# A decode kernel on one core: alignment branches ahead of the opening barrier on ScalarE, GpSimd and VectorE

## The chip, the cores and the metric

The kernel runs on one core of a Trainium2 chip. The metric is the device time of one execution in microseconds (us). Most executions of a kernel agree within 0.3%, but there is a second, slower state: here about 444.7 us instead of 436.4 us. Runs are compared fast with fast. The trace also gives a *span*, from the first to the last recorded instruction.

## The reference, cut to what matters

```python
mod = silu(c) @ w_mod                                  # (8, 1024) @ (1024, 6144): six modulation rows
h = layernorm(x) * (1 + ca) + sa
x = x + ga * attention(h, k_cache, v_cache, wq, wo)    # 8 batches, 32 query heads on 4 key heads, 8192 keys of 128
h = layernorm(x) * (1 + cb) + sb
x = x + gb * ((relu(h @ W_gate) * (h @ W_up)) @ W_down)
```

There is one new token per batch, so every weight and every cache entry is read once and used in little arithmetic: 185.6 MB come from HBM, the chip's main memory.

## The kernel before

A small recording layer collects every operation with what it reads and writes, works out the semaphores, and emits one program per engine. SyncE issues all large loads, in order, each as soon as the buffer that it overwrites has been read. The attention over eight batches is a loop on ScalarE, VectorE and TensorE. GpSimd has no loop: its eight products in the attention stand one after another.

The program opens with a barrier of all engines. Two helper steps matter here. The first moves the first loads ahead of that barrier, so that the stream starts at once (its first packet is at 1.01 us, and the barrier opens at 1.42 us):

```python
def start_loads_first(nc, n):
    ...
    for engine, ahead, total in ((mybir.EngineType.SP, 2, n), (mybir.EngineType.Activation, 2, 2)):
        ins = list(block.instructions)
        at = where(ins, engine, "EventSemaphore")[0]
        first = [ins[i] for i in where(ins, engine) if i > at][:total]
        ...
        rest = rest[:at] + first[ahead:] + rest[at:]
        at = where(rest, engine)[0]
        block.instructions = rest[:at] + first[:ahead] + rest[at:]
```

The second emits an engine's code ahead of the loop, and then the loop:

```python
        for x in engines:
            mine = [i for i, o in enumerate(self.ops) if o["eng"] == x]
            inside = [i for i in mine if self.ops[i]["trip"] is not None]
            after[x] = [self.ops[i] for i in mine if inside and i > inside[-1]]
            straight(x, [self.ops[i] for i in mine if not inside or i < inside[0]])
            ...
        with nc.Fori(0, len(self.trips["pe"]), engines=...) as self.turn:   # eight trips
            ...
```

ScalarE's two first loads are the small inputs `c` and `x` (16 KB each, tile `cx`). The first matmul needs both.

## Time and profile before

| what | number | where |
|---|---|---|
| device time, three runs before the prediction | 436.49, 436.64, 444.67 us | run list |
| profiled execution | 444.49 us, span 443.1 us, slow state | run list, page |
| DMA busy, 40 slices | 90% or more in 39 | page |
| share of the load queue | 98.9% of 16 engines' span | page |
| fetches of instructions in the span | five of 16 KiB, one of 8 KiB | packet records |

These lines are from the page of the kernel before, as it was profiled (in the slow state). The DMA row gives tenths of busy time in 40 slices. The queue lines give packets, MB, and the share of the sixteen engines' span.

```profile
span 443.1 us, 4774 instructions
...
DMA  9999999999999999999999999999999999999995
...
q1 hardware_dynamic: 5360, 185.61, 98.9%
q8 instruction: 5, 0.08, 0.1%
...
q14 instruction: 1, 0.01, 0.0%
```

The reader should see two things. The DMA engines are full for the whole span, nearly all of it with the one queue of large loads (q1). And two queues of kind "instruction" move a little as well (0.09 MB): I read these as the programs themselves being fetched.

Next, pieces of the chain of waits of the same profile, in order of time: start in us, duration in us, what.

```profile
381.51 24.74 DMA arena<-in_B_W_gate_dram
...
413.18 26.30 DMA arena<-in_B_W_down_dram
...
439.53 0.61 PE ps L763 x8
...
441.05 0.42 DVE ob L769
```

The chain ends in load landings. Only about 3.6 us of arithmetic and store follow the last landing in it.

The start of the same profile, from its timeline: start us, duration us, engine, line, operation, and in brackets the idle time before it and what ended it (`issue`: nothing that the profile shows; a name with `q`, such as `PEq`: that engine's sequencer, which issues its instructions; `DMA`: a landing).

```profile
0.00 1.44 SPq L391 DMA_DIRECT2D arena<-in_w_mod_dram  x3
0.12 0.40 ACTq L423 DMA_DIRECT2D cx<-in_c_dram  x1
0.23 0.10 POOL L794 MEMSET const-float32-0.0<- 128x1 f32 x1 [0.23 <-issue]
...
0.56 0.44 ACTq L423 DMA_DIRECT2D cx<-in_A_x_dram  x1
1.42 1.28 ACT L451 ACT_TABLE_LOAD   x1 [1.42 <-PEq L794]
...
1.57 0.34 SPq L391 DMA_DIRECT2D arena<-in_A_wq_dram  x1
...
10.03 0.58 PE L447 MATMUL ps<-cx,rsel 32*128 32x512 bf16 x1 [10.03 <-DMA cx<-in_A_x_dram]
```

SyncE queues three loads (12,288 KiB) at once. The barrier opens at 1.42 us, which ScalarE's table load shows. The first matmul waits for the small load of `x` until 10.03 us.

The trace also records each DMA packet. The fetches of instructions, as start in us and size, worked out from those records:

```
8 KiB:   84.7
16 KiB:  50.2  104.2  393.8  410.5  436.6
```

Last, the landing records hold sixteen times for each load, and a wait ends with the last of them. For the small load of `x` the median of the sixteen is 8.18 us and the last 9.94 us, and the matmul that waits for it starts at 10.03 us. For the gate load the median is 404.52 us and the last 406.26 us, and its wait in the chain ends at 406.25 us. I call one of the sixteen a *part*.

### The profile page before, as it was taken

The numbers are of one execution on the slowest core, as the hardware profiler recorded it, in microseconds if no ns is written. First come the engines' busy times: TensorE is split into PE (matmuls) and PEld (weight loads), VectorE is DVE, ScalarE is ACT, GpSimd is POOL, SyncE is SP. The second block draws the span as 40 slices with busy tenths as digits, with TensorE's granted clock in tenths as the row PEclk, the third lists the DMA queues.
The fourth block names the chain that finished last, engine by engine and source line by source line (L and its number), as shares of the span: only waits on it lengthen the run. The fifth ranks groups of instructions, "written<-read, shape, count | busy, mean of one in ns | idle before, by whom it ended". The sixth has DMA issues, their size and how long they took to land. (4 is left out here: it accounts for less than half of the span.)

```text
span 443.1 us, 4774 instructions
## 1 busy us (share of the span) xinstructions
PE 263.3 (59%) x2139; PEld 138.0 (31%) x1979; DVE 249.0 (56%) x342; ACT 29.5 (7%) x54; POOL 8.7 (2%) x22
## 2 busy tenths in 40 slices
PE   0324336728865783886578388658838865365157
PEld 0100002218225421822542172154217215241015
DVE  0603028872985697298569729756972975421020
ACT  1100010020001002000100200010020010100000
POOL 3000000000000000000000000000000000000000
PEclk9976657978996997799599889959968996865668
DMA  9999999999999999999999999999999999999995
GB/s 367 417 355 390 404 385 426 379 417 430 467 396 420 456 444 420 429 470 390 435 476 408 423 429 467 420 423 473 399 420 426 467 455 402 452 416 419 439 414 239
DMA packets 5494, 185.74 MB, mean 419 GB/s; under 512 B 656, under 2 KB 752, under 8 KB 1136
## 3 DMA queue, kind: packets, MB, share of 16 engines
q1 hardware_dynamic: 5360, 185.61, 98.9%
q8 instruction: 5, 0.08, 0.1%
q10 hardware_dynamic: 128, 0.04, 0.0%
q14 instruction: 1, 0.01, 0.0%
HBM read 185.63 MB, written 0.02 MB: 419 GB/s over the span
## 5 line engine op out<-in xcount | busy, mean ns | idle before, releaser
L576 DVE STREAM_TRANSPOSE kt<-arena 128x1024 uint32<-128x1024 uint32 x128 | 148.2, 1211 | 64.4 <-DVEq L181 47.3
L586 PE MATMUL ps<-kt,qpad 128*128 128x512 bf16 x512 | 133.9, 384 | 44.1 <-DVE kt L576 38.1
L626 PE MATMUL ps<-arena,pT 128*64 128x256 bf16 x1024 | 74.5, 320 | 51.8 <-PEq L181 51.8
L626 PEld LDWEIGHTS ps<-arena,pT 128*64 128x64 bf16 x1024 | 72.0, 132 | 53.7 <-issue 53.1
L586 PEld LDWEIGHTS ps<-kt,qpad 128*128 128x128 bf16 x512 | 40.5, 98 | 133.7 <-DVE kt L576 101.0
L616 DVE TENSOR_SCALAR pT<-pd,mqf 128x1024 bf16<-128x1024 bf16 x64 | 28.2, 503 | 0.6
L608 ACT ACTIVATE prb<-ps,bias 128x1024 bf16<-128x1024 f32 x16 | 17.7, 1109 | 139.8 <-DVE mjt L603 139.8
L614 DVE STREAM_TRANSPOSE pd<-prb 128x1024 bf16<-128x1024 bf16 x16 | 19.8, 1239 | 10.9 <-ACT prb L608 10.9
L592 DVE TENSOR_REDUCE negm<-ps 128x1 f32<-128x512 f32 x32 | 21.2, 661 | 4.5 <-PE ps L586 4.5
L744 PE MATMUL ps<-arena,hT 128*32 128x448 bf16 x128 | 11.1, 535 | 16.8 <-DMA arena<-in_B_W_up_dram 11.4
L751 DVE TENSOR_TENSOR kt<-ps,kt 128x448 bf16<-128x448 f32 x2 | 1.2, 618 | 27.6 <-PE ps L744 27.6
L514 PE MATMUL ps<-arena,hT 128*32 128x512 bf16 x96 | 10.3, 615 | 9.7 <-DMA arena<-in_w_mod_dram 9.7
L538 PE MATMUL ps<-arena,hT 128*32 128x512 bf16 x64 | 7.2, 631 | 14.6 <-DMA arena<-in_A_wq_dram 14.6
L645 ACT ACTIVATE oacc<-ps 128x32 f32 (+1 forms) x9 | 1.8, 197 | 159.4 <-PE ps L640 159.4
L521 DVE COPY mod<-ps 128x512 f32<-128x512 f32 x2 | 1.3, 670 | 19.3 <-PE ps L514 19.3
L567 POOL TENSOR_TENSOR qpad<-qR,mq 128x128 bf16<-128x128 bf16 x8 | 4.9, 608 | 319.2 <-DVE pT L616 260.8
L549 DVE CAST kt<-ps 128x512 bf16<-128x512 f32 x1 | 0.7, 691 | 18.2 <-PE ps L538 18.2
L744 PEld LDWEIGHTS ps<-arena,hT 128*32 128x32 bf16 x64 | 2.4, 140 | 25.7 <-DMA arena<-in_B_W_up_dram 12.0
L763 PE MATMUL ps<-arena,hmT 128*32 128x256 bf16 x112 | 8.3, 309 | 3.5 <-DVE hmT L754 3.1
L714 PE MATMUL ps<-arena,kt 128*32 128x256 bf16 x128 | 5.9, 373 | 5.1 <-DMA arena<-in_A_wo_dram 5.1
L598 PE MATMUL ps<-identf,negm 128*128 128x128 f32 x16 | 3.9, 326 | 7.8 <-DVE negm L596 7.8
L763 PEld LDWEIGHTS ps<-arena,hmT 128*32 128x32 bf16 x112 | 6.5, 109 | 5.6 <-DMA arena<-in_B_W_down_dram 4.9
(87 smaller groups left out, 80.9 us busy)
## 6 DMA issues: line engine op xcount, KB each, us to landing
arena<-in_A_k_cache_dram SPq DMA_DIRECT2D x16, 4096.0 KB, 27.5
arena<-in_A_wq_dram SPq DMA_DIRECT2D x2, 4096.0 KB, 38.3
arena<-in_B_W_gate_dram SPq DMA_DIRECT2D x1, 7168.0 KB, 24.7
arena<-in_B_W_up_dram SPq DMA_DIRECT2D x1, 7168.0 KB, 27.9
arena<-in_w_mod_dram SPq DMA_DIRECT2D x1, 6144.0 KB, 33.4
arena<-in_w_mod_dram SPq DMA_DIRECT2D x1, 5888.0 KB, 17.8
arena<-in_B_W_down_dram SPq DMA_DIRECT2D x1, 3584.0 KB, 19.7
arena<-in_B_W_down_dram SPq DMA_DIRECT2D x1, 1792.0 KB, 23.6
```

What stands on the lines that cost most here:

```text
L514: fns.append(lambda e, w=w, pr=pr, j=j, kk=kk: hold(e.matmul(ps[32 * j:32 * j + 32, pr, :], hT[:, kk, :], w[:, 2 * pr:2 * pr + 2, j, :], s ...
L538: fns.append(lambda e, w=w, r=kk - r0, z=z, g=g, kk=kk: hold(e.matmul(ps[32 * g:32 * g + 32, 4 + z, :], hT[:, kk, :], w[:, r, g, z, :], st ...
L576: P.op("dve", lambda e_: e_.transpose(ktb[:, to:to + PART].bitcast(dt.uint32), arena[:, lo:lo + PART].bitcast(dt.uint32)), reads=[slot_r(l ...
L586: fns.append(lambda e_, t=t, r=r: e_.matmul(ps[:, e // 4, :].rearrange("p (c k) -> p c k", k=32), qpad[:, t * 2 + r, 24 - 8 * i:152 - 8 * ...
L592: P.op("dve", lambda e: e.tensor_reduce(negm[:, h:h + 1], ps[:, h, :], AX.X, ALU.max, negate=True), reads=[bank(h)] + (free(("ka", b)) if ...
L608: P.op("act", lambda e: e.activation(prb[:, f, :], ps[:, 2 * f:2 * f + 2, :].rearrange("p h n -> p (h n)"), ACT.Exp, bias=bias[:, 0:1], sc ...
L614: P.op("dve", lambda e: e.transpose(pd[:, f], prb[:, f]), reads=[R("prb", f, f + 1)], writes=[R("pd", 1024 * f, 1024 * f + 1024)])
L616: P.op("dve", lambda e, g=g: e.tensor_scalar(out=pT[:, f, :, :, g, :], in0=pd[:, f].rearrange("p (c i x) -> p c i x", c=32, i=2), scalar1= ...
L626: fns.append(lambda e, n=n, h=h, c_=c_, i=i, t=t: e.matmul(ps[64 * t:64 * t + 64, 5, 0:2 * Dh].rearrange("p (i d) -> p i d", d=Dh), pT[:, ...
L714: fns.append(lambda e, w=w, k=k, j=j: e.matmul(ps[32 * j:32 * j + 32, 5, 0:256], oX[:, k, :], w[:, k, j, :], start=(k == 0), stop=(k == KO ...
L744: fns.append(lambda e, w=w, kk=kk, h=h, j=j, b0=b0: hold(e.matmul(ps[32 * j:32 * j + 32, b0 + h, 0:H], hT[:, kk, :], w[:, kk, j, h, :], st ...
L763: fns.append(lambda e, w=w, r=k - r0, k=k, i2=i2, j=j: e.matmul(ps[32 * j:32 * j + 32, 4, 0:256], hmT[:, k, 1 - i2:33 - i2], w[:, r, i2, j ...
```

## The change

The intent is in its short description: ScalarE, GpSimd and VectorE branch to their next fetch block ahead of their opening-barrier instructions, ScalarE behind its two loads. A fetch block is the stretch of instructions that one fetch brings. So, as it is meant, the fetch of the block that follows happens at the start, and the rest of a short program lies in one block. The 128 is the change's own figure; how many instructions an 8 KiB fetch holds was not measured.

```diff
+    ALIGNED = dict(act=128, pool=128, dve=128)
 ...
         after = {}
+        self.aligns = []
         for x in engines:
+            if x in self.ALIGNED:
+                self.aligns.append(engines[x].addr_align(self.ALIGNED[x], offset=0, max_nops=0))
             mine = [i for i, o in enumerate(self.ops) if o["eng"] == x]
 ...
+def align_first(nc, aligns):
+
+    block = nc.main_func.blocks[0]
+    names = {x.ins.name for x in aligns}
+    ins = list(block.instructions)
+    rest = [x for x in ins if x.name not in names]
+    for a in ins:
+        if a.name in names:
+            at = next(i for i, x in enumerate(rest) if x.engine == a.engine)
+            rest.insert(at, a)
+    block.instructions = rest
 ...
         P.emit(nc, dict(sp=nc.sync, act=nc.scalar, pool=nc.gpsimd, dve=nc.vector, pe=nc.tensor), sems)
+        align_first(nc, P.aligns)
         start_loads_first(nc, 3)
```

With no padding instructions allowed (`max_nops=0`), the padding up to the boundary is branched over.

## The prediction

> **What bounds the kernel.** DMA. The profile page moves 185.7 MB at a mean 419 GB/s; its DMA row is 9 (90% or more) in 39 of 40 slices, and the load queue alone takes 98.9% of the sixteen engines' span. The chain of waits ends in two load landings (gate 24.7 us, down 26.3 us) with about 3.5 us of PE, DVE and store behind them. (The profiled run was slow; fast ones take 436.5 us.) At the head, the issue list shows three modulation-weight loads (12.3 MB, the last landing at 34.5 us) and the next one at 1.57 us, so the queue never runs dry.
>
> **What the change does.** Each of ScalarE, GpSimd and VectorE gets one alignment instruction ahead of its opening barrier (ScalarE behind its two small loads); the rest is unmoved. Their code then starts on a block. VectorE has about 103 instructions in the built program, ScalarE 32, GpSimd 29, so each should fit in one block.
>
> [...] The packet records show five 16 KiB fetches, at 50.2, 104.2, 393.8, 410.5 and 436.6 us (I read them as TensorE's), and one of only 8 KiB[...] at 84.7 us (I read it as VectorE crossing a block in its first loop trip). No wait list shows a stall by them.
>
> They cost DMA time: after 50.2 us one of the sixteen landings of every load comes about 1.7 us behind the mean of the others (spread 0.59 us for the load landing at 45.3, 2.15 at 57.6); after 104.2 another is 1.35 behind; the 84.7 us fetch puts a third about 0.5 behind. A load is complete when its slowest part is, so the end is set by the parts that TensorE's fetches delay, which the change leaves alone. Removing the 84.7 us fetch helps a part that is not last: about 0, at best 0.3 us.
>
> **Cost.** Three branches, and probably three 8 KiB fetches in the first 2 us (each 0.36 to 0.59 us by the packet records) (the stream's first packet is at 1.0 us). One that collides puts up to 0.6 us on one DMA engine, which reaches the end only if that engine is last. A late barrier, even by 2 to 4 us, is hidden: the first matmul waits for the second small load until 10.0 us, when GpSimd (2.6 us) and ScalarE (2.7 us) are long ready; the next large load, at 1.57 us, has some 30 us of queue ahead of it.
>
> **Predicted:** 436.6 us, 434.6 to 440.0. Faster by over 2%: 0.02; within 2%: 0.95; slower: 0.03.
>
> **What would show it.** Right: the 8 KiB fetch at 84.7 us gone; three 8 KiB fetches near 0 to 3 us; the five 16 KiB ones still at the same places; the 0.5 us laggard landing gone but the 1.7 us one still there; barrier end (ScalarE's first table load, 1.42 us) 0.3 to 4 us later, the first matmul still near 10 us. Wrong: a first matmul after 20 us, a DMA share under 0.9 in the first 40 us, or 8 KiB fetches repeating each loop trip.
>
> **What would make it wrong.** A fetch stuck behind the loads that holds the barrier over 30 us; a new fetch falling on the DMA engine that is already last (+0.5 us); most of the runs falling in the slow state (about 444.5 us).

That each of the three programs fits in one block was the author's estimate; after the change no 8 KiB fetch comes later than 5.9 us. The forecast's sum starts from the 436.5 us of the fast runs of before, takes about 0 off for VectorE's fetch (at best 0.3 us), counts up to 0.6 us for a collision only on the part that is last, and comes to 436.6 us.

## More of the kernel before

GpSimd's program starts with four tiny memsets of constants ahead of the barrier (at 0.23 to 0.34 us in the trace).

GpSimd's first memset is at 0.23 us.

## The result, and the profile after

The changed kernel takes a median of 435.89 us (435.68 to 436.63, six runs, all fast). The kernel before takes 436.56 us (436.25 to 444.67, six runs). The ratio of the fast runs is 0.9988, with a 95% interval of 0.9974 to 1.0001. That ratio is the mean time of one kernel's fast runs over the mean of the other's in the same rounds, so it is not quite the ratio of the two medians. Neither kernel is faster by 2%. If there is a difference, it is about 0.5 us.

The page of the changed kernel:

```profile
span 435.2 us, 4777 instructions
...
DMA  9999999989999999999999999999999999999995
...
q1 hardware_dynamic: 5360, 185.61, 98.9%
q8 instruction: 5, 0.08, 0.1%
...
q14 instruction: 3, 0.02, 0.0%
```

Its chain of waits, the pieces that answer to those above:

```profile
374.29 23.93 DMA arena<-in_B_W_gate_dram
...
404.38 27.18 DMA arena<-in_B_W_down_dram
...
431.60 0.62 PE ps L780 x8
...
433.13 0.42 DVE ob L786
```

And its start, from the timeline:

```profile
0.00 1.44 SPq L408 DMA_DIRECT2D arena<-in_w_mod_dram  x3
0.12 0.40 ACTq L440 DMA_DIRECT2D cx<-in_c_dram  x1
0.56 0.44 ACTq L440 DMA_DIRECT2D cx<-in_A_x_dram  x1
0.66 0.10 POOL L812 MEMSET const-float32-0.0<- 128x1 f32 x1 [0.66 <-issue]
...
1.79 1.28 ACT L468 ACT_TABLE_LOAD   x1 [1.79 <-PEq L812]
...
1.79 0.33 SPq L408 DMA_DIRECT2D arena<-in_A_wq_dram  x1
...
10.32 0.58 PE L464 MATMUL ps<-cx,rsel 32*128 32x512 bf16 x1 [10.32 <-DMA cx<-in_A_x_dram]
```

The span is 7.9 us shorter than in the profile before, but this compares a slow run with a fast one and says nothing about the change. A fast profile of before was needed, and the first experiment provides it. What can be read here is the start. The barrier opens at 1.79 us instead of 1.42, GpSimd's first memset is at 0.66 us instead of 0.23, and the first matmul is at 10.32 us. The queue q14 has three fetches in the span instead of one. By the packet records they lie at 2.0, 2.2 and 5.9 us, and the one in the middle of the run is gone. The five 16 KiB fetches are still there.

### The profile page after: what moved, and what is told of

Read it like the earlier page. It is cut to its first block, busy times and chain, and to the rows that moved or that the text cites. A ratio compares the mean times of both kernels' runs of the same rounds, so it can differ in the third digit from the quotient of the medians.

```text
span 435.2 us, 4777 instructions
## 1 busy us (share of the span) xinstructions
PE 261.1 (60%) x2139; PEld 138.0 (32%) x1979; DVE 248.9 (57%) x342; ACT 29.5 (7%) x54; POOL 8.8 (2%) x22
## 3 DMA queue, kind: packets, MB, share of 16 engines
q1 hardware_dynamic: 5360, 185.61, 98.9%
## 5 line engine op out<-in xcount | busy, mean ns | idle before, releaser
L643 PE MATMUL ps<-arena,pT 128*64 128x256 bf16 x1024 | 76.5, 326 | 50.7 <-PEq L182 50.7
L643 PEld LDWEIGHTS ps<-arena,pT 128*64 128x64 bf16 x1024 | 73.8, 134 | 52.8 <-issue 52.0
L761 PE MATMUL ps<-arena,hT 128*32 128x448 bf16 x128 | 9.2, 461 | 19.7 <-DMA arena<-in_B_W_up_dram 12.3
L584 POOL TENSOR_TENSOR qpad<-qR,mq 128x128 bf16<-128x128 bf16 x8 | 4.9, 609 | 310.8 <-DVE pT L633 257.9
L731 PE MATMUL ps<-arena,kt 128*32 128x256 bf16 x128 | 4.9, 329 | 4.6 <-DMA arena<-in_A_wo_dram 4.6
## 6 DMA issues: line engine op xcount, KB each, us to landing
arena<-in_B_W_gate_dram SPq DMA_DIRECT2D x1, 7168.0 KB, 23.9
```

The costliest lines, as they stand in the source:

```text
L584: P.op("pool", lambda e: e.tensor_tensor(out=qpad[:, :, 24:152].rearrange("p u (q c) -> p u q c", q=4)[:, :, :, 0:J], in0=qR[:].rearrange( ...
L643: fns.append(lambda e, n=n, h=h, c_=c_, i=i, t=t: e.matmul(ps[64 * t:64 * t + 64, 5, 0:2 * Dh].rearrange("p (i d) -> p i d", d=Dh), pT[:, ...
L761: fns.append(lambda e, w=w, kk=kk, h=h, j=j, b0=b0: hold(e.matmul(ps[32 * j:32 * j + 32, b0 + h, 0:H], hT[:, kk, :], w[:, kk, j, h, :], st ...
```

## The experiments

The questions were two. Is the small gain of 0.5 us real, and where is it? And is it true that a fetch costs DMA time, but that this reaches the end only through the slowest part?

A number used throughout is device time minus span. The run list gives both for every run, in the changed kernel 0.85 to 0.94 us and in the profiled run of before 1.35 us. That made me suspect that the gain lies outside the span.

### Before once more, and one engine at a time

`e1_null` is the kernel before with one comment added. `e2`, `e3` and `e4` are the changed kernel with one engine aligned:

```diff
-    ALIGNED = dict(act=128, pool=128, dve=128)
+    ALIGNED = dict(dve=128)     # e2;  act=128 in e3;  pool=128 in e4
```

> The kernel before once more, unchanged but for a comment. It gives a fast profile of before, which the record lacks (its profiled run was slow), and the noise of the comparison. Every theory: ratio 1.000, interval within 0.001 either way. Theory A (the small gain is outside the span of first to last instruction): time minus span is about 1.35 us here as in the profiled run before, against 0.85 to 0.94 us in the changed kernel's runs. Theory B (the gain lies in the load stream, by the fetch at 84.7 us gone): time minus span is the same as in the changed kernel and the span itself is about 0.5 us longer. Theory C (noise): neither differs by more than 0.2 us.

> Only VectorE is aligned; its 8 KiB fetch in the loop goes. Theory B: the whole gain of about 0.5 us stays. Theory A: the gain stays only if VectorE's place in its block is what costs time outside the span; the time minus span tells. Theory C: ratio within 0.001 of 1.

> Only ScalarE is aligned, so VectorE's fetch at about 80 us must be back in the packet records. Theory B: no gain, 0.0 us. Theory A: whichever of the three single engines shows the shorter time minus span (0.9 instead of 1.35 us) carries the gain. Theory C: ratio within 0.001 of 1.

> Only GpSimd is aligned; VectorE's fetch at about 80 us is back, and the barrier opens about 0.4 us later than before. Theory B: no gain. Theory A: as for the other single engines, time minus span tells. Theory C: ratio within 0.001 of 1.

The fast profile of before (`e1_null`), lines of its page and then of its timeline:

```profile
span 435.1 us, 4774 instructions
...
DMA  9999999999999999999999999999999999899995
...
q14 instruction: 1, 0.01, 0.0%
```

```profile
0.23 0.10 POOL L794 MEMSET const-float32-0.0<- 128x1 f32 x1 [0.23 <-issue]
...
1.41 1.28 ACT L451 ACT_TABLE_LOAD   x1 [1.41 <-PEq L794]
...
8.56 0.58 PE L447 MATMUL ps<-cx,rsel 32*128 32x512 bf16 x1 [8.56 <-DMA cx<-in_A_x_dram]
```

Means over the fast runs of each kernel. The column before the last is device time minus span, and the last is the start of the first instruction that the profile counts as work (neither DMA issue nor semaphore), from the profile:

| kernel | device time | span | time minus span | first work at |
|---|---|---|---|---|
| before, 10 runs beside e1 to e4 | 436.39 | 435.06 | 1.33 | 0.23 |
| changed, 6 runs | 436.00 | 435.10 | 0.90 | 0.66 |
| e2, VectorE only, 5 runs | 436.53 | 435.22 | 1.31 | 0.23 |
| e3, ScalarE only, 4 fast runs | 436.35 | 435.00 | 1.35 | 0.23 |
| e4, GpSimd only, 5 runs | 436.14 | 435.24 | 0.90 | 0.66 |

The null kernel gave a median of 436.35 us. One of its six runs was at 440.56 us, and it widens the interval of the ratio to 0.9985 to 1.0048. Its other runs lie between 436.11 and 436.48 us.

The spans agree within 0.24 us. The packet records show VectorE's fetch in e1 (77.0 us), e3 (76.7 us) and e4 (76.9 us), and none in e2. So taking that fetch away (e2) gains nothing, and theory B falls. GpSimd alone shortens time minus span by 0.43 us, as much as all three engines together. (Its device time is only 0.25 us below that of before, because its mean span came out 0.18 us longer.) Theory A stands, in the form that concerns GpSimd.

### What GpSimd's alignment does to the measured time

Two readings were left. In A1, the device time counts from the first work on any engine. The alignment delays GpSimd's first memset, which is that first work, by 0.43 us. In A2, GpSimd's place in its block really saves time at the start or the end.

`e5_pool_behind` keeps the branch, but behind the four memsets:

```diff
             at = next(i for i, x in enumerate(rest) if x.engine == a.engine
+                      and (a.engine != mybir.EngineType.Pool or x.opcode == "Drain"))
```

> The changed kernel, but GpSimd's alignment stands behind its four small memsets instead of ahead of them; its branch, block and fetch stay, and so do the other two engines'. GpSimd's first memset should be back at 0.23 us (0.66 in the changed kernel). Theory A1 (the measured time starts with the first non-DMA work on an engine, which is GpSimd's first memset; delaying that by 0.43 us is the whole gain): time minus span returns from 0.9 to about 1.33 us, and the time to about 436.35, with the span as before. Theory A2 (GpSimd's place in its fetch block saves the time, at the start or the end of the program): time minus span stays at 0.9 us and time near 435.9.

`e6_early_dve` leaves GpSimd as in the changed kernel, and adds one useless VectorE memset as the first work of the program:

```diff
+            if x == "dve":
+                self.early = engines[x].memset(self.scratch[:, 0:1], 0.0)   # moved to the front of VectorE's program
```

> The changed kernel with one tiny VectorE memset of a scratch column put ahead of VectorE's alignment, so that it is the first work of the program (about 0.1 to 0.3 us); GpSimd is untouched and still starts at 0.66 us. Theory A1: time minus span goes from 0.9 back to about 1.3 to 1.45 us, span unchanged, time about 436.35. Theory A1' (only GpSimd's own start counts): time minus span stays at 0.9. Theory A2: stays at 0.9.

`e12_pool_two` adds a second alignment on GpSimd, to the middle of the same block:

```diff
+                if x == "pool":
+                    self.second = engines[x].addr_align(128, offset=64, max_nops=0)
+                    self.aligns.append(self.second)          # stands behind the first one
```

> The changed kernel with a second alignment behind GpSimd's first, to the middle of the same block: one more branch, no new block. GpSimd's first memset moves from 0.66 to 0.9 to 1.1 us. Theory A1: time minus span is 1.55 minus the start of the first memset, so 0.45 to 0.65 us, span 435.1 as before, time 435.5 to 435.75: lower than both kernels with no work done sooner. Rival A2: 0.9 and 436.0 as in the changed kernel.

The first work in the timelines of e5, e6 and e12:

```profile
0.23 0.10 POOL L813 MEMSET const-float32-0.0<- 128x1 f32 x1 [0.23 <-issue]
```

```profile
0.14 0.06 DVE L213 MEMSET scratch<- 128x1 f32 x1
...
0.66 0.10 POOL L819 MEMSET const-float32-0.0<- 128x1 f32 x1 [0.66 <-issue]
```

```profile
0.81 0.10 POOL L815 MEMSET const-float32-0.0<- 128x1 f32 x1 [0.81 <-issue]
```

| kernel | device time, mean of fast runs | span | time minus span | first work at | sum of the last two |
|---|---|---|---|---|---|
| before | 436.39 | 435.06 | 1.33 | 0.23 | 1.56 |
| changed | 436.00 | 435.10 | 0.90 | 0.66 | 1.56 |
| e5 | 436.40 | 435.10 | 1.30 | 0.23 | 1.53 |
| e6 | 436.64 | 435.23 | 1.41 | 0.14 | 1.55 |
| e12, five runs | 436.83 | 436.08 | 0.75 | 0.81 | 1.56 |

The rows come from three rounds, which the record lists under different chips; before's own time minus span was 1.30 us beside e5 and e6 and 1.34 us beside e12. The sum is constant within 0.03 us. So the device time is the span, less what passes ahead of the first work, plus about 1.55 us. In e6 the first work stands on VectorE, and time minus span went up by 0.51 us against the changed kernel (the time by 0.64 us, of which 0.13 us are the span). In e5 all three branches stayed and the gain was gone (median 436.45 us, before in the same round 436.42). A2 falls.

The chip was restless in the round of e12: one of its runs took 486.37 us, one 440.15 (in the mean of the table), and a run of before took 442.15. The ratio of the fast runs is 1.0000, with an interval of 0.9944 to 1.0056, so the time itself shows nothing here, and its median of 436.29 us lies outside the 435.5 to 435.75 that I expected. The three quietest runs of e12 took 435.64, 435.78 and 435.82 us, the quietest of before 436.11 to 436.19. My expectation of 0.9 to 1.1 us for the first memset was too late. The second branch cost only 0.15 us (0.81 less 0.66), while the first, by its edit into another block, cost 0.43 (0.66 less 0.23). With the measured 0.81, time minus span is what A1 demands.

So e12's quiet runs are about 0.4 us below those of before, and it does no work sooner. They are no faster than the three quietest of the changed kernel (435.68, 435.77 and 435.85 us): the 0.15 us between these two shows in time minus span (0.75 against 0.90) and not in the time. e12 is no better version. It shows what the 0.5 us of the change are made of.

### Is the head on the path?

`e8_act_ahead` puts ScalarE's alignment ahead of its two loads:

```diff
         start_loads_first(nc, 3)
+        align_first(nc, P.aligns[:1])
```

> The changed kernel with ScalarE's alignment ahead of its two small loads. They are issued about 0.4 us later (0.12 and 0.56 us in the changed kernel), so they meet the stream that starts at 1.0 us. The first matmul, which waits for them, starts 0 to 2 us later than the 10.3 us of the changed kernel. My theory: hidden, span and time within 0.3 us of the changed kernel, time minus span 0.9. Rival (the head is on the path): the span grows by as much as the first matmul is late.

From its timeline:

```profile
0.57 3.67 ACTq L440 DMA_DIRECT2D cx<-in_c_dram  x1
...
4.28 0.45 ACTq L440 DMA_DIRECT2D cx<-in_A_x_dram  x1
5.14 1.28 ACT L468 ACT_TABLE_LOAD   x1 [5.14 <-PEq L813]
...
18.15 0.58 PE L464 MATMUL ps<-cx,rsel 32*128 32x512 bf16 x1 [18.15 <-DMA cx<-in_A_x_dram]
```

The issue of the first small load took 3.67 us (0.40 in the changed kernel), and the second was issued at 4.28 us behind 12.6 MB of large loads. The barrier opened at 5.14 us, and the first matmul started at 18.15 us, 7.8 us later than in the changed kernel and well beyond the 2 us that I had allowed for. Yet the mean span is 435.20 us and the time 436.10 us (four fast runs; before in the same round 435.04 and 436.34 us, ratio 0.9996, 0.9980 to 1.0011, which the record classes as unclear). The head has at least about 7.8 us of slack, within the 0.2 us by which mean spans scatter. That is why the placement behind the loads, sensible as it is, does not show in the time either. Why that load's issue took 3.67 us is not settled.

### What does a fetch cost in the load stream?

`e7_dose32` puts four aligned branches ahead of each of GpSimd's eight products, each followed by a one-column memset:

```diff
+            far = []
+            for i in range(4):
+                far += [lambda e: e.addr_align(128, offset=0, max_nops=0),
+                        lambda e, i=4 * b + i: e.memset(scratch[:, i:i + 1], 0.0)]
-            P.op("pool", lambda e: e.tensor_tensor(
+            P.op("pool", far + [lambda e: e.tensor_tensor(
```

> The changed kernel with four more aligned branches on GpSimd ahead of each of its eight in-loop products, 32 in all, each followed by a one-column memset: 32 more 8 KiB fetches while the load stream runs. Theory R (fetches are spread over the sixteen DMA engines): two more per engine, about 2 x 0.3 to 0.55 us, so the span grows by 0.6 to 1.2 us, and the spread of a load's sixteen landings stays at 2 to 3 us. Theory S (fetches of one engine's code go through one DMA engine): that one falls 32 x 0.3 to 0.55 = 10 to 17 us behind and the span grows by about that. Theory N (fetches cost nothing): span within 0.3 us.

GpSimd's timeline in the second trip, and then the longest of TensorE's waits (total us, times, longest):

```profile
100.07 0.32 POOL L588 MEMSET scratch<- 128x1 f32 x1 [24.01 <-DVE pT L638]
105.83 0.10 POOL L588 MEMSET scratch<- 128x1 f32 x1 [5.44 <-issue]
111.32 0.10 POOL L588 MEMSET scratch<- 128x1 f32 x1 [5.39 <-issue]
114.41 0.10 POOL L588 MEMSET scratch<- 128x1 f32 x1 [2.99 <-issue]
114.47 0.46 POOL L589 TENSOR_TENSOR qpad<-qR,mq 128x128 bf16<-128x128 bf16 x1
```

```profile
PE ps L608 <- POOL qpad L589: 69.4, 8, 20.4
```

The span grew to 459.0 us in the mean, by 23.9 us: more than any of the three theories said (the time is 1.053 of before's, 1.051 to 1.055; the record classes it as unclear). The experiment measured something else as well. Such a branch, with its fetch, mostly takes about 5.5 us while the stream runs (of the 24 gaps between memsets of one trip most are 5.2 to 5.8 us; the shortest, the last one above, is 3.1 us and the longest 6.7). Four of them ahead of the product made TensorE wait 69.4 us in all for `qpad`. It was not a clean test of a fetch's DMA cost. What it did show in the landing records is that of a load's sixteen parts, one alone fell behind, by more than 5 us at times, while from 135 us on the second latest stayed within 0.7 us of the median until the loop ended.

`e9_dose32_late` puts the same branches behind each product, where GpSimd idles anyway (310.8 us ahead of the eight products in the changed kernel):

```diff
                  reads=[R("qR"), R("mq"), R("qpad")], writes=[R("qpad")])
+            for i in range(4):                     # range(1) in e10
+                P.op("pool", [lambda e: e.addr_align(128, offset=0, max_nops=0),
+                              lambda e, i=4 * b + i: e.memset(scratch[:, i:i + 1], 0.0)])
```

> The 32 extra GpSimd branches once more, but behind each qpad product instead of ahead of it, so that the 22 us or so that four of them take (5.5 us each in e7) pass while GpSimd would idle and no engine waits for them. In e7 each fetch put one and the same landing part about 0.65 us further behind. Theory S (all of GpSimd's fetches go through one DMA engine, which cannot catch up): that part ends 32 x 0.65 = about 21 us behind the others and the span grows by roughly 15 to 20 us (TensorE's 1.5 to 2 us lag is covered by it). Theory R (spread over the engines): span grows by at most 1.3 us. Theory N (only stalls cost, fetches do not): span within 0.3 us of 435.1.

> The same with one branch per trip, eight in all. Theory S: 8 x 0.65 = 5.2 us of lag on one part, against the 1.5 to 2 us that TensorE's fetches leave on another, so the span grows by about 3 to 3.7 us; not 5.2, because the first 1.5 to 2 us are covered. Theory R and N: within 0.5 us.

GpSimd's timeline of e9, second trip. The product now comes first and waits only for VectorE:

```profile
88.64 0.62 POOL L585 TENSOR_TENSOR qpad<-qR,mq 128x128 bf16<-128x128 bf16 x1 [13.04 <-DVE pT L637]
89.21 0.38 POOL L592 MEMSET scratch<- 128x1 f32 x1
94.91 0.10 POOL L592 MEMSET scratch<- 128x1 f32 x1 [5.32 <-issue]
100.51 0.10 POOL L592 MEMSET scratch<- 128x1 f32 x1 [5.51 <-issue]
106.02 0.10 POOL L592 MEMSET scratch<- 128x1 f32 x1 [5.41 <-issue]
```

No wait of TensorE names GpSimd any more. Still the mean span is 456.05 us, 20.95 us more than in the changed kernel, that is 0.65 us for each of the 32 fetches. In e10 it is 439.53 us (three fast runs), 4.43 us more for eight fetches. Before's fast runs of the same round have a mean span of 435.18 us without the disturbed one, so the growth is not the restless round. (e9: ratio 1.0457, and e10: 1.0071 with an interval of 1.0002 to 1.0140.) The rivals allowed at most 1.3 us for e9. In e10, the lag behind the median of the latest part, for the second K load of successive batches, is as follows (worked out from the landing records):

```
batch        1     2     3     4     5     6     7
lag, us   1.80  2.42  3.04  3.56  3.81  4.45  5.65
```

That is 0.64 us per trip in the mean (3.85 us in six steps of 0.25 to 1.20), with one fetch per trip, and on one part alone. The second latest part stays between 1.2 and 1.8 us behind. So theory S holds for GpSimd: its fetches all delay the same part. (The records do not name the part; that it is the same one is inferred from a lag that adds up.) The packet of such a fetch is recorded with only 0.31 us (e10), half of the lag that it leaves; where the other half comes from was not studied. Both growths are somewhat above my figures (15 to 20, and 3 to 3.7 us). For e10 I had left out GpSimd's fetch at the start, which delays the same part if S holds. With it, nine fetches of 0.65 us less the 1.42 us by which the changed kernel's last load is late anyway come to 4.4 us, an estimate that agrees. In e9 the latest part is only 5.2 us behind at the end, not 21. My reading is that the next loads wait for buffers that the late part holds up, so that the other fifteen idle with it. It fits that the load queue's share of the engines falls from 98.9% in the changed kernel to 95.7% in e9 (from these shares, an estimate of 15 us more idle time for each engine), but the link was not traced.

`e11_pe_too` aligns TensorE too, ahead of its barrier and to a multiple of 256 instructions, and so moves its fetches:

```diff
-    ALIGNED = dict(act=128, pool=128, dve=128)
+    ALIGNED = dict(act=128, pool=128, dve=128, pe=256)
```

> The changed kernel with TensorE aligned too[...]. Its block crossings move by the rest of the first block: the fetch at 45.9 us should go (an early one near 1 to 3 us in its place) and the next ones come at other times, the first mid-stream one in the first loop trip, 60 to 90 us. Theory S: the part that is 1.9 us behind from the load landing at 52.5 us on appears only after the new first mid-stream fetch; at the end some part is still 1.2 to 1.8 us behind, so span within 0.5 us of 435.1 and time minus span 0.9. Rival (the lag comes from something else at 46 us than the fetch): the lag still starts with the load that lands at 52.5 us.

Its 16 KiB fetches lie at 2.1, 62.3, 98.6, 385.5, 402.5 and 429.9 us; those of the changed kernel at 45.9, 96.3, 385.5, 402.6 and 428.3. How far the three latest parts of a load are behind the median of its sixteen, in us, from the landing records:

```
                    second wq load        second K load,       last W_down
                    (lands near 52 us)    batch 1 (110 us)     (432 us)
before (e1)         0.13 0.13 1.97        1.03 1.56 1.85       1.53 1.55 1.75
changed             0.55 0.64 1.95        0.47 1.38 1.71       1.20 1.22 1.42
e2, VectorE only    0.22 0.64 2.03        0.58 1.56 1.96       1.32 1.46 1.78
e11                 0.71 0.82 1.44        1.21 1.21 1.23       1.07 1.12 1.22
```

In the changed kernel one part is suddenly 1.95 us late with the load after the fetch at 45.9 us. In e11 that fetch is gone. The load that lands near 42 us, ahead of it, already has a part 1.44 us late (0.66 in the changed kernel), and no jump follows at 52 us. I had expected the lag only after the first fetch in mid-stream (62.3 us); it is there from the large load that lands at 18.3 us on (1.45 us), after TensorE's early fetch at 2.1 us. The lag goes with the fetch. At the end several parts are late by 1.1 to 1.2 us, and the mean span is 435.14 us, as in the changed kernel. In both kernels the fetches fall on several parts. But from before to changed to e11 the latest part's lag at the end falls from 1.75 to 1.42 and 1.22 us, and the mean span does not fall with it (435.06, 435.10, 435.14). So the lag behind the median is not by itself time that can be gained. The second column also shows what I read as VectorE's fetch: a part 1.03 us late in before, while the third latest is 0.47 us late in the changed kernel and 0.58 in e2. It was never the latest.

So in these records a fetch delays one part of the sixteen. How a fetch and the large loads share an engine was not shown.

## Why the prediction was right

- **DMA bounds the kernel.** Right. In the fast profile of before, the DMA row is 9 in all slices but two, one of them the last.
- **No gain from VectorE's fetch.** Right, and shown by e2: without that fetch, the span is 435.22 us against 435.06. The size of its lag was off (I said 0.5 us; the fast profile shows 1.03), but the step holds, as that part is not the last one.
- **The end is set by TensorE's fetches, which stay.** In two halves. That the latest part sets the end is shown: in all fourteen profiles the last matmul ends 0.44 us after the latest landing of the W_down loads, and in e9 and e10 a part that does become the latest lengthens the run. That TensorE's fetches are what makes it late is supported: the 1.9 us lag starts with the fetch at 45.9 us and moves with it in e11. But e11 left the span as it was, and whether the kernel would gain anything without TensorE's fetches was not tried.
- **The late barrier is hidden.** Right. The barrier opened 0.37 us later, and in e8, with the first matmul 7.8 us later, the span did not change.
- **Three 8 KiB fetches in the first 3 us.** Two, at 2.0 and 2.2 us. The third, at 5.9 us, is ScalarE's (e3, with ScalarE alone, has one at 6.0 us). It does no harm.
- **436.6 us.** 435.89, inside the range and 0.7 us lower. What the prediction did not have is the only thing that was shown to move the time: GpSimd's first memset starts 0.43 us later, and the device time counts from the first work. e5 and e6 show it by taking the gain away, e12 by the time minus span. The forecast is in effect the time of before unchanged, so the close number says little for the mechanism by itself; the runs above do.
- **Open:** whether the span itself differs by 0.1 or 0.2 us, since fast runs of one kernel scatter more than that; what lies in the 1.55 us between the measures; and the cause of the slow state, which was not studied.

## What to carry to other kernels

When the gain of a change at the start of a program is below a microsecond, look at which event the clock starts with: a delay of the first counted work looks like a gain (0.43 us here, in time minus span). In this kernel, which DMA bounds, code fetched in the middle of the stream delayed one of the sixteen parts of the loads, by about 0.65 us for each fetch of 8 KiB in the mean of e9 (VectorE's single fetch left a part 1.03 us late in e1) and by about 1.5 us for one of 16 KiB (an estimate from e1, where the latest part goes from 0.43 us behind, just ahead of the fetch, to 1.97). It lengthened the run here only when that part became the latest (e10, against e2), so count the late parts ahead of removing a fetch. Placing a short program in one block did neither harm nor good here. By these runs it could pay only where an engine waits for a fetch or a fetch delays the latest part, and no run here has such a case.

What these runs measured of fetches and branches, and of the reported time:

- TensorE's fetches are 16 KiB, those of ScalarE, GpSimd and VectorE 8 KiB (e11; e3, e7 and e2). In the kernel before and in the changed one no wait of an engine was traced to a fetch.
- Branches from block to block in quick sequence mostly took about 5.5 us each under a full stream (e7, e9; 3.1 to 6.7).
- At the start of the program, an alignment branch delayed GpSimd's first memset by 0.15 us where its edit stays within a block (e12) and by 0.43 us where it goes to the next (the changed kernel).
- In every kernel run here the reported time fits a start at the first instruction that counts as work, not at the first DMA issue: time minus span plus the start of that work is 1.53 to 1.58 us.
